# Second product with the tokens as output rows, one store for each block of tokens, squares in pairs, 64-column attention tiles, and a new order of all engines

## The chip, the cores and the metric

The kernel runs on one core of one Trainium2 chip. A core has a matrix engine (PE, with its weight loads shown apart as PEld), a vector engine (DVE), a scalar engine (ACT), a general engine (POOL) and a queue engine (SP), which here issues most of the DMA transfers. The engines run side by side and wait for each other by semaphores. The metric is the time of one execution on the device in microseconds. Names such as `h`, `r`, `g`, `o` are the program's tiles; L576 means line 576 of the kernel before.

## The reference

```python
def phi(x):                                   # r = 8 sketches, S1 and S2 are 8 x 32
    a = np.einsum('rd,bhsd->bhsr', S1, x)
    b = np.einsum('rd,bhsd->bhsr', S2, x)
    return np.einsum('bhsi,bhsj->bhsij', a, b).reshape(*x.shape[:-1], r * r)
q_p, k_p = (phi(q), phi(k))                   # batch 4, heads 4, seq 1088, head_dim 32
kv = np.einsum('bhsf,bhsd->bhfd', k_p, v)
z = np.sum(k_p, axis=2)
num = np.einsum('bhsf,bhfd->bhsd', q_p, kv)
den = np.einsum('bhsf,bhf->bhs', q_p, z)[..., None] + 1e-06
x = (num / den)                               # to 4352 tokens x 128
h = x @ w_in                                  # 128 x 2048
r = np.maximum(h, 0.0)
g = r * r
return (g @ w_out).astype(np.float32)         # 2048 x 128
```

All inputs and the output are float32. The attention is computed in float32, the two large products from bfloat16 operands.

## The kernel before

There are two parts that overlap. **Attention** goes through four batches. For each it loads k, q and v, transposes k and q on DVE (`tk`, `tq`, lines 343, 345 and 409), multiplies k with the sketches on PE (`ksk`, line 359), copies one sketch on ACT (`ka`, line 364) and multiplies the two on DVE (`kp`, line 372). `kv` (line 388) sums k features times v over the sequence in one PSUM tile; `kve` (line 401) copies the sum to SBUF. The q features of batches 0 and 1 are made in the same way (`qr` on PE, line 423; `qa` on ACT, line 435; `qp` on DVE, line 440); those of batches 2 and 3 go through DRAM: `qr` (line 452), one copy `ab` (line 459), four writes `wr`, several reads `rda` and `rdb` that spread the rows, and one DVE product (line 489). `num` (line 521) multiplies q features with `kv`, `mx` (lines 533 to 535) divides by the denominator on DVE, `tx` (line 548) transposes the quotient on PE, and `xe` (line 553) copies it to `xT`, which holds x with the 128 features as partitions and the tokens as columns.

A matrix product in float32 shows in the profile as two passes, each with a weight load of its own. The output rows of `ksk`, `kv` and `num` are cut into column tiles of 32 (`KSK_M`, `KV_M`, `NUM_M`), so that four small products stand side by side in the array.

**The two large products** go through nine blocks of tokens (384, seven times 512, 384). A block has eight steps. A step multiplies two 128-column pieces of `w_in` with the block's tokens (`m1`, line 576, two matmuls of 512 or 384 columns into an `h` tile), takes the maximum with zero (`r`, ACT line 588 or DVE line 590), squares (`g`, DVE line 603 or ACT line 601), and adds to the block's output (`m2`, line 609). In `m2` the weights `w_out` are the stationary operand and `g` streams, so the output tile `o` holds the 128 output features as partitions and the tokens as columns. `oe` (line 616) transposes 32 x 32 squares from `o` to an output tile on DVE, and four stores a block (more where a block crosses a batch), each with runs of 32 floats, bring it to DRAM (line 626).

The order is written out by hand as a table, `PLAN`: each entry names an operation, its engine and the buffers that it takes. Each engine runs its entries in the order of the table, so an entry that waits holds up all entries of its engine behind it. There are three `h` tiles, one `a`, one `o` (each in PSUM), five `r` and five `g` tiles. A transfer of the two hardware DMA queues (those that SP and ACT issue) takes one of eight semaphores in turn and so waits for the landing of the transfer eight before it. Fourteen matmuls with zeros (`heat`) fill PE at the start.

Of the kernel before, what the change touches and what calls it, by code (L numbers as in the profile page):

```python
# [44 lines left out]
ldv0.0:SP SR1:POOL heat10:PE heat11:PE heat12:PE ldv0.1:ACT ksk0.1:PE:h0 ldv1.2:SP ldv1.0:SP ka0.1:ACT tq0.0:DVE kp0.1:DVE qr0.1:PE:h1:h2 gate:POOL
ksk0.0:PE:a0 qa0.1.0:ACT:A0 qp0.1.0:DVE ka0.0:ACT qr0.0:PE:h0:h1 qa0.1.1:ACT:A1 vp0.0:POOL vp0.1:POOL kp0.0:DVE kv0.0:PE:a0 kv0.1:PE qa0.0.1:ACT:A2
qp0.0.1:DVE qp0.1.1:DVE kz0:POOL qa0.0.0:ACT:A0 ldk1.0:SP kve0.2:ACT ldv1.3:SP qp0.0.0:DVE qr0.2:PE:h1:h2 kve0.1:ACT kve0.0:DVE kz1:POOL tk1.0:DVE
ldq2.0:SP kve0.3:ACT num0.0:PE:h0 qa0.2.0:ACT:A2 num0.1:PE:a0 warm:ACT qp0.2.0:DVE mx0.0:DVE:den0 ksk1.0:PE:h1 z1:POOL tx0.0:PE:h0 heat13:PE
qa0.2.1:ACT:A1 mx0.1:DVE:den1 win1:POOL ka1.0:ACT tx0.1:PE:a0 xe0.0:ACT m1.0.2:PE:h0 win2:POOL ldv1.1:SP xe0.1:ACT win0:POOL qp0.2.1:DVE tq2.0:DVE
m1.0.3:PE:h2 ksk1.1:PE:a0 r.0.2:ACT:r0 r.0.3:ACT:r1 ldv1.t:SP qr2:PE:h0 m1.0.4:PE:h2 ldq1.0:SP kp1.0:DVE num0.2:PE:h1 ka1.1:ACT ab2:ACT r.0.4:ACT:r2  # L50
m1.0.7:PE:h0 kz3:POOL kp1.1:DVE m1.0.0:PE:h2 vp1.0:POOL kv1.0:PE:a0 wr2.2:SP r.0.7:ACT:r3 mx0.2:DVE:den2 wout0:POOL tx0.2:PE:h1 wout1:POOL
r.0.0:ACT:r4 m1.0.6:PE:h0 xe0.2:ACT g.0.4:DVE:g0 r.0.6:ACT:r2 vp1.1:POOL m1.0.1:PE:h2 m1.0.5:PE:h1 wout2:POOL g.0.2:DVE:g1 g.0.3:DVE:g2 kv1.1:PE
m1.1.4:PE:h0 g.0.0:DVE:g3 m2.0.0:PE:o0 ldv2.2:SP tq1.0:DVE r.0.1:ACT:r0 ldv2.0:SP r.0.5:ACT:r1 r.1.4:DVE:r4 g.0.1:ACT:g4 qr1.0:PE:h2:h1 m2.0.1:PE
m1.1.0:PE:h0 m2.0.2:PE m2.0.3:PE wr2.1:SP ldq3.0:SP g.0.7:DVE:g3 kve1.0:DVE qa1.0.0:ACT:A0 qa1.0.1:ACT:A2 kve1.3:DVE qp1.0.0:DVE m1.1.1:PE:h2
r.1.0:ACT:r0 g.0.5:DVE:g4 m2.0.4:PE g.0.6:ACT:g1 g.1.0:ACT:g2 qp1.0.1:DVE qr1.1:PE:h0:h1 qa1.1.0:ACT:A1 wr2.0:SP m2.0.5:PE r.1.1:DVE:r3 kve1.1:DVE
kve1.2:DVE ldv2.1:SP qa1.1.1:ACT:A0 ldk2.0:SP m1.1.2:PE:h2 num1.0:PE:a0 g.1.4:DVE:g0 r.1.2:ACT:r1 rdb2.0.1.0:SP g.1.1:ACT:g4 m2.0.6:PE qp1.1.1:DVE
# [629 lines left out]
```

## Time and profile before

| What | us |
|---|---|
| median of 3 runs | 120.26 |
| lowest and highest run | 119.08 and 120.42 |
| profiled execution, first to last instruction | 119.9 |
| PE busy | 101.0 (84%) |
| DVE busy | 94.6 (79%) |
| ACT busy | 85.0 (71%) |
| POOL busy | 15.1 (13%) |
| DMA queues issued by SP, ACT and POOL, share of 16 engines | 44.9%, 2.0%, 5.8% |

The page gives the profiled execution no other time than its span, which lies within the three runs. Busy shares are means over three stages with different limits: a head, in which the first batch's attention is loaded and computed, a long middle, in which PE works almost without a pause, and a tail with the last stores. The chain of waits follows back what ended last; rows by line give the number of instructions, their busy time and the mean duration of one; rows by stretch give the busy time of each engine within it.

### The profile page before, as it was taken

Reading aid. Unit: us, or ns where it says so; the run is one execution under the profiler, and the core shown is the slowest. Engines: PE = TensorE matmul, PEld = TensorE weight load, DVE = VectorE, ACT = ScalarE, POOL = GpSimd, SP = SyncE. Lnnn points to the kernel's source line nnn. Section 1 sums busy time; section 2 is a strip of 40 time slices with the busy share of each in tenths; the row PEclk is TensorE's granted clock in tenths of the full one; section 3 lists DMA queues with packets and bytes.
Section 4 is the critical chain, followed back from the end, with each engine's and each line's share of the span. In section 5 each row is a group of like instructions: output and inputs, shape, how many; then the busy total and the mean of one; then the engine's idle time right before and its main releaser. Section 6 shows DMA issues by size and latency. Waiting matters only on the chain.

```text
span 119.9 us, 4646 instructions
## 1 busy us (share of the span) xinstructions
PE 101.0 (84%) x2002; PEld 59.2 (49%) x2002; DVE 94.6 (79%) x154; ACT 85.0 (71%) x117; POOL 15.1 (13%) x45
## 2 busy tenths in 40 slices
...
GB/s 92 354 201 276 296 231 133 91 5 23 208 291 185 142 250 77 88 201 94 249 211 163 223 162 125 107 93 0 0 0 0 27 109 26 48 68 84 58 73 36
DMA packets 26596, 15.29 MB, mean 127 GB/s; under 512 B 19792, under 2 KB 24272, under 8 KB 26576
## 3 DMA queue, kind: packets, MB, share of 16 engines
q1 hardware_dynamic: 23808, 13.39, 44.9%
...
q10 hardware_dynamic: 1776, 0.56, 2.0%
...
HBM read 13.25 MB, written 2.79 MB: 134 GB/s over the span
## 4 chain that ended last, share of the span: by engine, by line
PE 67%; DMA 10%; issue 6%; DVE 4%; ACT 3%; ACTq 2%; SPq 1%; POOL 1%; DVEq 0%
PE h L576 24%; PE o L609 21%; DMA vin<-in_v_dram 10%; PE h L521 6%; PE a L388 4%; PE a L521 3%; PE h L548 2%; PE h L359 2%; PE h L452 2%; ACT g L601 2%; ACTq L211 2%; PE h L423 1%; ACT r L588 1%; PE a L359 1%; DVE g L603 1%
## 5 line engine op out<-in xcount | busy, mean ns | idle before, releaser
L588 ACT ACTIVATE r<-h 128x1024 bf16<-128x1024 f32 (+1 forms) x60 | 55.3, 978 | 4.2 <-PE h L576 2.5
L609 PE MATMUL o<-g,w_out 128*128 128x512 bf16 (+1 forms) x144 | 39.9, 368 | 0.7 <-DVE g L603 0.5
L576 PE MATMUL h<-xT,w_in 128*128 128x512 bf16 (+1 forms) x144 | 39.6, 369 | 0.3 <-ACT xT L553 0.2
L603 DVE TENSOR_TENSOR g<-r 128x1024 bf16<-128x1024 bf16 (+1 forms) x54 | 34.0, 670 | 0.4
L576 PEld LDWEIGHTS <-w_in 128*128 128x128 bf16 x144 | 15.6, 115 | 14.2 <-issue 1.4
L609 PEld LDWEIGHTS <-w_out 128*128 128x128 bf16 x144 | 13.3, 98 | 14.6 <-issue 1.8
L601 ACT ACTIVATE g<-r 128x1024 bf16<-128x1024 bf16 (+1 forms) x18 | 17.4, 994 | 0.6 <-PE o L609 0.4
L590 DVE TENSOR_SCALAR r<-h 128x1024 bf16<-128x1024 f32 (+1 forms) x12 | 13.7, 1153 | 0.4 <-PE h L576 0.2
L329 POOL COPY vp<-vin 128x512 f32<-128x512 f32 x8 | 5.8, 737 | 44.8 <-DMA vin<-in_v_dram 44.8
L521 PE MATMUL h<-kvz,qp 128*32 128x66 f32 x304 | 6.7, 223 | 5.1 <-issue 4.6
L521 PEld LDWEIGHTS h<-kvz,qp 128*32 128x32 f32 x304 | 5.5, 110 | 6.9 <-issue 5.8
L388 PEld LDWEIGHTS a<-vp,kp 128*32 128x32 f32 x576 | 6.3, 113 | 3.7 <-issue 3.7
L388 PE MATMUL a<-vp,kp 128*32 128x33 f32 x576 | 7.2, 202 | 0.8 <-issue 0.8
L343 DVE STREAM_TRANSPOSE kT<-kin 128x1024 f32<-128x1024 f32 (+1 forms) x5 | 5.0, 1010 | 3.4 <-DMA kin<-in_k_dram 3.4
L364 ACT COPY ka<-h 128x160 f32<-128x160 f32 (+1 forms) x4 | 1.1, 283 | 9.3 <-PE h L359 9.3
L616 DVE STREAM_TRANSPOSE osb<-o 128x512 f32<-128x512 f32 (+1 forms) x9 | 6.1, 683 | 1.7 <-PE o L609 1.7
L435 ACT COPY A<-h 128x384 f32<-128x384 f32 (+1 forms) x12 | 5.2, 462 | 2.5 <-PE h L423 2.5
L440 DVE TENSOR_TENSOR qp<-h,A 128x384 f32<-128x384 f32 (+1 forms) x12 | 6.0, 524 | 0.9 <-ACT A L435 0.9
L423 PE MATMUL h<-qT,SR 32*64 32x192 f32 (+1 forms) x192 | 6.4, 359 | 0.3 <-DVE qT L409 0.3
L359 PE MATMUL h<-SK,kT 128*32 128x64 f32 x152 | 3.5, 240 | 3.4 <-DVE SK L226 3.4
L257 PE MATMUL o<-zero 128*128 128x512 bf16 x14 | 4.8, 505 | 1.2 <-DVE zero L205 1.2
L372 DVE TENSOR_TENSOR kp<-h,ka 128x1280 f32<-128x1280 f32 (+1 forms) x4 | 5.6, 1403 | 0.0
...
## 6 DMA issues: line engine op xcount, KB each, us to landing
...
```

The source lines that it names most:

```text
L359: nc.tensor.matmul(o[m * g : m * g + m, :, j - j0, :], kT[i][:, c : c + m], SK.rearrange("p x h r -> p x (h r)"), start=True, stop=True)
L388: nc.tensor.matmul(at(vb)[p : p + m, 33 * (h // 2) : 33 * (h // 2) + 33], kp[i][:, j, 64 * h + m * f : 64 * h + m * f + m], vp[i][:, h, j, :],
L423: nc.tensor.matmul(at(hb[h // 2])[lo : lo + 64, 512 * half + 256 * x : 512 * half + 256 * x + n], SR[32 * h : 32 * h + 32, x].rearrange("p ...
L440: nc.vector.tensor_tensor(out=qp[i][:, pr, t0 : t0 + 2 * n].rearrange("p (m s) -> p m s", m=2), in0=at(hb[pr]).rearrange("p (m s) -> p m s ...
L521: nc.tensor.matmul(t[32 * cc : 32 * cc + 32 * w, 2 * pr : 2 * pr + 2, :], qp[i][:, pr, 32 * c : 32 * c + 32 * w], (kvs if sw else kvz)[b][ ...
L576: nc.tensor.matmul(at(hb)[:, col(w) : col(w) + N], w_in[:, 512 * (ct // E) : 512 * (ct // E) + 512].rearrange("p (c e) -> p e c", e=E)[:, ...
L588: nc.scalar.activation(o, i_, ACTF.Relu)
L590: nc.vector.tensor_scalar_max(o, i_, 0.0)
L601: nc.scalar.activation(at(gb)[:, 0:tot], r, ACTF.Square)
L603: nc.vector.tensor_tensor(out=at(gb)[:, 0:tot], in0=r, in1=r, op=ALU.mult)
L609: nc.tensor.matmul(at(ob)[:, 0:N], w_out[:, ct, :], at(gb)[:, W * N * (mm % SQ_W) + N * w : W * N * (mm % SQ_W) + N * w + N], start=(ct == ...
L616: nc.vector.transpose(at(sbuf)[:, 0:N], at(ob)[:, 0:N])
```

## The change

In `m2` the operands change places: pieces of 128 tokens of `g` become the stationary operand and `w_out` streams, 128 columns at a time. One matmul of 512 columns becomes four of 128 columns, each with a weight load of its own, and the output tile has tokens as partitions. `m1` reads the tokens in another sequence (runs of 32 columns), chosen so that a partition of the output tile holds neighbouring rows of the output. `oe` becomes a plain copy on ACT or DVE, and a block is stored by one transfer with runs of up to 2 KB (a few where a block crosses a batch) instead of four or more with runs of 128 B. Squares of the seven 512-token blocks are taken over two steps at once (2048 columns), with four `r` tiles and three `g` tiles of twice the size. The column tiles of `ksk`, `kv` and `num` are 64 wide. The sketches are the first loads of ACT's queue, v of batch 0 is loaded by SP, and one of the two small sketch copies moves from POOL to ACT. The table `PLAN` is new for all engines.

```diff
--- before.py
+++ after.py
@@ -16,14 +16,15 @@
 N_H = 3
 N_A = 1
 N_O = 1
-NR = 5
-SQ_W = 1
-N_OSB = 4
+N_R = 4
+N_G = 3
+SQ_W = (1, 2, 2, 2, 2, 2, 2, 2, 1)
+N_OSB = 3
 N_DEN = 3
 N_AA = 3
 N_HEAT = 14
-NUM_M = (32, 32, 32, 32)
-S_ENG = "ACT"
+NUM_M = (64, 64, 64, 64)
+S_ENG = "ACT|SP"
 W_PARTS = ((0, 1), (1, 2), (2, 4))
 MODE = ('pe', 'pe', 'dma', 'dma')
 Q_LOADS = (((0, 12), (12, 34)), ((0, 34),), ((0, 34),), ((0, 34),))
@@ -32,63 +33,57 @@
 KVS = (((0, 4), (4, 9)), ((0, 4), (4, 9)), ((0, 4), (4, 9)), ((0, 4), (4, 9)))
 RD_PARTS = (((0, 768), (768, 1088)), ((0, 768), (768, 1088)), ((0, 768), (768, 1088)), ((0, 768), (768, 1088)))
 SIZES = [384, 512, 512, 512, 512, 512, 512, 512, 384]
-KSK_M = (32, 32, 32, 32)
-KV_M = (32, 32, 32, 32)
+KSK_M = (64, 64, 64, 64)
+KV_M = (64, 64, 64, 64)
 V_ENG = "SP|ACT"
 RDB_ENG = "SP"
+ST_ENG = "SP"
 K_LOADS = (((0, 16), (16, 34)), ((0, 34),), ((0, 34),), ((0, 34),))
 
 
 PLAN = """
-iota:POOL ldv0.3:ACT zero:DVE heat0:PE:o0 heat1:PE heat2:PE heat3:PE z0:POOL mk:POOL heat4:PE lds1:ACT ldk0.16:SP tk0.16:DVE ldk0.0:SP lds0:ACT
...
+zero:DVE heat0:PE:o0 heat1:PE heat2:PE z1:POOL kz2:POOL mk:POOL ldq0.0:SP tq0.0:DVE lds1:ACT lds0:ACT trS:DVE ldk0.16:SP tk0.16:DVE ldk0.0:SP SK:DVE
...
 """
 
 
@@ -150,9 +145,9 @@
         tiles[f"a{i}"] = PS(f"a{i}", 512)
     for i in range(N_O):
         tiles[f"o{i}"] = PS(f"o{i}", 512)
-    for i in range(NR):
-        tiles[f"r{i}"] = T(f"r{i}", [128, 1024 * SQ_W], BF16)
-        tiles[f"g{i}"] = T(f"g{i}", [128, 1024 * SQ_W], BF16)
+    for kind, count in (("r", N_R), ("g", N_G)):
+        for i in range(count):
+            tiles[f"{kind}{i}"] = T(f"{kind}{i}", [128, 1024 * max(SQ_W)], BF16)
     for i in range(N_OSB):
         tiles[f"osb{i}"] = T(f"osb{i}", [128, 512])
     for i in range(N_DEN):
@@ -560,12 +555,14 @@
         last = None
         W = 4 if N <= 256 else 2
         per = 512 // N if N <= 256 else 1
+        sq = SQ_W[n]
+        X = N // 128
         for m in range(CT // W):
-            if m % SQ_W == 0:
+            if m % sq == 0:
                 rb, gb = Buf("r"), Buf("g")
                 o_r = []
             hb = Buf("h")
-            off = W * N * (m % SQ_W)
+            off = W * N * (m % sq)
 
             def col(w, N=N, per=per):
                 return 512 * (w // per) + N * (w % per)
@@ -576,7 +573,7 @@
                     nc.tensor.matmul(
                         at(hb)[:, col(w) : col(w) + N],
                         w_in[:, 512 * (ct // E) : 512 * (ct // E) + 512].rearrange("p (c e) -> p e c", e=E)[:, ct % E],
-                        xT[:, n0 : n0 + N], start=True, stop=True)
+                        xT[:, n0 : n0 + N].rearrange("p (c x t) -> p x c t", x=X, t=32), start=True, stop=True)
             wi = o_win[wpart(W * m + W - 1)]
             wo = o_wout[wpart(W * m + W - 1)]
             o1 = add(f"m1.{n}.{m}", "PE", f_m1, deps + [wi], alloc=[hb], n=W * N)
@@ -588,12 +585,12 @@
                     nc.scalar.activation(o, i_, ACTF.Relu)
                 else:
                     nc.vector.tensor_scalar_max(o, i_, 0.0)
-            new = m % SQ_W == 0
+            new = m % sq == 0
             o_r.append(add(f"r.{n}.{m}", "ACT|DVE", f_r, [o1], alloc=[rb] if new else [], uses=[hb] if new else [hb, rb], n=W * N,
                            after=[] if new else o_r[:1]))
-            if m % SQ_W < SQ_W - 1:
+            if m % sq < sq - 1:
                 continue
-            tot = W * N * SQ_W
+            tot = W * N * sq
 
             def f_g(e, rb=rb, gb=gb, tot=tot):
                 r = at(rb)[:, 0:tot]
@@ -602,32 +599,42 @@
                 else:
                     nc.vector.tensor_tensor(out=at(gb)[:, 0:tot], in0=r, in1=r, op=ALU.mult)
             o3 = add(f"g.{n}.{m}", "DVE|ACT", f_g, o_r, alloc=[gb], uses=[rb], n=tot)
-            for mm in range(m - SQ_W + 1, m + 1):
+            for mm in range(m - sq + 1, m + 1):
                 def f_m2(e, mm=mm, gb=gb):
                     for w in range(W):
                         ct = W * mm + w
-                        nc.tensor.matmul(at(ob)[:, 0:N], w_out[:, ct, :],
-                                         at(gb)[:, W * N * (mm % SQ_W) + N * w : W * N * (mm % SQ_W) + N * w + N],
-                                         start=(ct == 0), stop=(ct == CT - 1))
+                        lo = W * N * (mm % sq) + N * w
+                        for x in range(X):
+                            nc.tensor.matmul(at(ob)[:, 128 * x : 128 * x + 128], at(gb)[:, lo + 128 * x : lo + 128 * x + 128], w_out[:, ct, :],
+                                             start=(ct == 0 and x == 0), stop=(ct == CT - 1), skip_group_check=True)
                 last = add(f"m2.{n}.{mm}", "PE", f_m2, [o3, wo, last], alloc=[] if mm else [ob], uses=[gb, ob] if mm else [gb], n=W * N)
         sbuf = Buf("osb")
 
         def f_oe(e):
-            nc.vector.transpose(at(sbuf)[:, 0:N], at(ob)[:, 0:N])
-        o_oe = add(f"oe{n}", "DVE", f_oe, [last], alloc=[sbuf], uses=[ob], n=N)
-        lo = n0
-        while lo < n0 + N:
-            b = lo // S
-            hi_ = min(n0 + N, S * (b + 1))
-            c0, c1 = (lo - S * b) // 32, (hi_ - S * b) // 32
-            for db in range(4):
-                def f_st(e, db=db, lo=lo, hi_=hi_, b=b, c0=c0, c1=c1):
-                    en = nc.sync if e == "SP" else nc.scalar
-                    en.dma_start(
-                        out=out[S * b : S * b + S, :].rearrange("(t c) d -> t c d", c=C)[:, c0:c1, 32 * db : 32 * db + 32],
-                        in_=at(sbuf)[32 * db : 32 * db + 32, lo - n0 : hi_ - n0].rearrange("p (c d) -> p c d", d=32))
-                add(f"st{n}.{lo}.{db}", "SP|ACT" if n == len(SIZES) - 1 else "SP", f_st, [o_oe], uses=[sbuf], n=128 * (hi_ - lo))
-            lo = hi_
+            fn = nc.scalar.copy if e == "ACT" else nc.vector.tensor_copy
+            fn(at(sbuf)[:, 0:N], at(ob)[:, 0:N])
+        o_oe = add(f"oe{n}", "DVE|ACT", f_oe, [last], alloc=[sbuf], uses=[ob], n=N)
+        c0, runs = n0 // 32, []
+        for g in range(4):
+            lo = c0 + X * g
+            while lo < c0 + X * g + X:
+                hi_ = min(c0 + X * g + X, C * (lo // C + 1))
+                if hi_ - lo == X and runs and runs[-1][3] - runs[-1][2] == X * runs[-1][1] and runs[-1][3] % C:
+                    runs[-1][1] += 1
+                    runs[-1][3] = hi_
+                else:
+                    runs.append([g, 1, lo, hi_])
+                lo = hi_
+        for i, (g, k, lo, hi_) in enumerate(runs):
+            def f_st(e, g=g, k=k, lo=lo, hi_=hi_):
+                en = {"SP": nc.sync, "ACT": nc.scalar, "POOL": nc.gpsimd}[e]
+                b, w = lo // C, (hi_ - lo) // k
+                x0 = lo - c0 - X * g
+                en.dma_start(
+                    out=out[S * b : S * b + S, :].rearrange("(t c) d -> t c d", c=C)[:, lo - C * b : hi_ - C * b].rearrange(
+                        "t (k x) d -> k t (x d)", k=k),
+                    in_=at(sbuf)[32 * g : 32 * g + 32 * k, 128 * x0 : 128 * x0 + 128 * w])
+            add(f"st{n}.{i}", ST_ENG if n < len(SIZES) - 1 else "SP|ACT", f_st, [o_oe], uses=[sbuf], n=16384 * (hi_ - lo))
 
     for b in range(B):
         attention(b)
@@ -635,7 +642,7 @@
     for n, N in enumerate(SIZES):
         ffn(n, n0, N)
         n0 += N
-    assert n0 == N_TOK
+    assert n0 == N_TOK and len(SQ_W) == len(SIZES)
 
     if not PLAN.strip():
         raise Planless(ops, slots)
```

How the order moves is shown at three places. The first is ACT's queue at the start; `S_sb` holds the sketches, `vin` is v of batch 0. Before:

```order
L314 DMA vin_114<-in_v_dram 32x4x256
L211 DMA S_sb<-in_S_dram 64x1x32 x2
L314 DMA vin_114<-in_v_dram 32x4x256 x2
L364 ACT_TABLE_LOAD
L364 COPY ka_128<-h_63 128x160
```

And in the changed kernel:

```order
L206 DMA S_sb<-in_S_dram 64x1x32 x2
L230 ACT_TABLE_LOAD
L230 COPY SR<-ST 128x64
L430 COPY A_87<-h_65 128x384
L430 COPY A_88<-h_63 128x384
```

The sketch loads now stand ahead of everything on ACT, and the three loads of v have left it for SP. The second place is DVE ahead of the first division `den`, `rec`, `xs`, on which the first `m1` depends (`kp` are the k features, `qp` the q features, `kT` and `qT` the transposed inputs). Before:

```order
L440 TENSOR_TENSOR qp_138<-h_65,A_92 128x384
L440 TENSOR_TENSOR qp_138<-h_63,A_91 128x384
L401 COPY kvz_132<-a_66 64x2x33
L343 STREAM_TRANSPOSE kT_123<-kin_107 128x1024
L345 STREAM_TRANSPOSE kT_123<-kin_107 128x64
L440 TENSOR_TENSOR qp_138<-h_64,A_93 128x320
L533 TENSOR_SCALAR den_82<-h_63 128x12
L534 RECIPROCAL rec_83<-den_82 128x12
L535 TENSOR_TENSOR xs_84<-h_63,rec_83 128x384
```

And in the changed kernel:

```order
L367 TENSOR_TENSOR kp_126<-a_66,ka_124 128x1024
L435 TENSOR_TENSOR qp_134<-h_63,A_88 128x320
L404 STREAM_TRANSPOSE qT_121<-qin_107 128x1088
L435 TENSOR_TENSOR qp_134<-h_64,A_89 128x384
L435 TENSOR_TENSOR qp_134<-h_65,A_87 128x384
L404 STREAM_TRANSPOSE qT_120<-qin_108 128x1088
L216 TENSOR_SCALAR ident<-iot 128x128
L528 TENSOR_SCALAR den_78<-a_66 128x12
L529 RECIPROCAL rec_79<-den_78 128x12
L530 TENSOR_TENSOR xs_80<-a_66,rec_79 128x384
```

The transposes of q of batches 1 and 2 and the making of `ident` now stand ahead of the first division, and the transpose of k of batch 1 has moved behind it. The third place is the end of SP's queue, the last stores (`osb` are the output tiles). Before:

```order
L626 DMA out_dram<-osb_79 32x8x32
L626 DMA out_dram<-osb_78 32x16x32 x4
L626 DMA out_dram<-osb_81 32x6x32
L626 DMA out_dram<-osb_79 32x8x32 x4
L626 DMA out_dram<-osb_80 32x12x32
```

And in the changed kernel:

```order
L633 DMA out_dram<-osb_75 32x512
L633 DMA out_dram<-osb_75 2x32x512
L633 DMA out_dram<-osb_76 4x32x512
L633 DMA out_dram<-osb_75 32x256
L633 DMA out_dram<-osb_77 4x32x384
```

Eleven stores of 32-float runs, with three more on ACT's queue, stand at the end before; in the changed kernel five stores of long runs do, and the last block's is a single one.

More of the change, by code (lines that the diff above doesn't have):

```diff
@@ L45 @@
[L45 to L56, printed above, removed]
@@ new lines @@
+iota:POOL win0:POOL ident:DVE kve0.1:ACT kve0.3:ACT kve0.0:ACT kve0.2:ACT num0.0:PE:a0 mx0.0:DVE:den0 qa1.1.1:ACT:A2 qp1.1.1:DVE qr2:PE:h2 heat11:PE
+heat12:PE wout0:POOL win1:POOL qa1.1.0:ACT:A0 qp1.1.0:DVE tk1.0:DVE ab2:ACT wr2.3:SP tx0.0:PE:a0 xe0.0:ACT qr1.2:PE:h1:h2 ldv1.0:SP ldv1.3:SP
+qa1.2.1:ACT:A1 qp1.2.1:DVE qa1.2.0:ACT:A2 ldv1.2:SP qp1.2.0:DVE heat13:PE m1.0.0:PE:h0 ksk1.0:PE:a0 r.0.0:ACT:r3 ka1.0:ACT kp1.0:DVE g.0.0:DVE:g0
+m1.0.4:PE:h2 r.0.4:ACT:r0 ksk1.1:PE:h1 ldv1.1:SP ka1.1:ACT m1.0.7:PE:h0 r.0.7:ACT:r1 m1.0.3:PE:h2 r.0.3:ACT:r2 kp1.1:DVE num0.1:PE:a0 mx0.1:DVE:den0
@@ new lines @@
+m1.0.2:PE:h0 r.0.2:ACT:r3 m2.0.0:PE:o0 num0.2:PE:h2 mx0.2:DVE:den1 qr1.0:PE:h0:h1 g.0.4:ACT:g1 qa1.0.0:ACT:A0 qp1.0.0:DVE kz3:POOL vp1.0:POOL
+kv1.0:PE:a0 ldv1.t:SP vp1.1:POOL qa1.0.1:ACT:A1 kv1.1:PE m1.0.1:PE:h2 qp1.0.1:DVE g.0.3:ACT:g2 kve1.0:DVE kve1.1:ACT kve1.3:ACT kve1.2:ACT tx0.2:PE:h0
+xe0.2:DVE r.0.1:ACT:r2 tx0.1:PE:h1 xe0.1:ACT num1.1:PE:a0 g.0.1:ACT:g0 m1.0.6:PE:h0 r.0.6:ACT:r0 ldk2.0:SP m1.0.5:PE:h2 r.0.5:ACT:r2 wr2.1:SP
+ldq3.0:SP num1.0:PE:h1 m2.0.1:PE g.0.2:ACT:g0 ldv2.0:SP wr2.0:SP tq3.0:DVE qr3:PE:h0 ab3:ACT mx1.1:DVE:den2 mx1.0:DVE:den1 m1.1.0:PE:h2 wr2.2:SP
@@ new lines @@
+wout1:POOL m2.0.2:PE g.0.7:DVE:g0 tk2.0:DVE r.1.0:ACT:r3 m1.1.2:PE:h1 r.1.2:ACT:r1 num1.2:PE:a0 mx1.2:DVE:den0 m1.1.3:PE:h0 r.1.3:ACT m1.1.1:PE:h2
+tx1.0:PE:h1 xe1.0:DVE m2.0.3:PE g.0.5:ACT:g2 r.1.1:ACT wout2:POOL m2.0.4:PE m1.1.6:PE:h0 rda2.0.1:SP m1.1.4:PE:h1 r.1.4:ACT:r2 ldv3.t:SP ldv2.2:SP
+g.0.6:DVE:g1 m2.0.5:PE rdb2.768.1.1:SP r.1.6:DVE:r0 ldv2.1:SP rdb2.0.1.0:SP ldv2.3:SP vp2.0:POOL m2.0.6:PE rda2.0.0:SP wr3.0:SP ldk3.0:SP m2.0.7:PE
+oe0:DVE:osb1 tx1.1:PE:a0 xe1.1:ACT m1.1.5:PE:h2 wr3.2:SP ldv3.3:SP r.1.5:ACT g.1.1:DVE:g1 m1.2.4:PE:h0 rdb2.0.0.0:SP tx1.2:PE:h1 xe1.2:ACT ldv2.t:SP
```

65 lines of the change are left out of this document (29 added, 36 removed).

## The prediction

> **What bounds the kernel now.** I read the page first (span), then the busy time by stretch, then the chain of waits.
>
> ```profile
> span 119.9 us, 4646 instructions
> ...
> 0.00:18.00 18.00, 12.18 (x350) 7.43 (x350) 8.91 (x17) 4.63 (x13) 7.89 (x32) 0.91 0.86 241
> 18.00:21.53 3.53, 0.00 (x1) 0.01 (x2) 0.95 (x3) 0.41 (x2) 1.84 (x5) 0.96 0.94 129
> ...
> 25.48:105.44 79.96, 78.44 (x1510) 45.19 (x1510) 75.25 (x117) 73.68 (x95) 5.34 (x9) 1.00 0.49 117
> 105.44:112.71 7.27, 6.59 (x34) 3.12 (x32) 6.32 (x10) 5.51 (x7) 0.00 (x0) 1.00 0.48 82
> ```
>
> A row by stretch has its length, then PE, PEld, DVE, ACT and POOL busy, the granted clock, and the DMA share with its GB/s. From 25.48 to 105.44 PE works 78.44 of 79.96 us (98%), DVE 94%, ACT 92%: the middle is PE's. The head is 25.48 us long, and 7.2 us are left of the span after the last matmul at 112.71. The chain of waits says what holds the head:
>
> ```profile
> 17.35 0.65 PE h L521 x25
> 18.00 3.53 issue
> ...
> 24.95 0.49 ACT xT L553
> 25.48 0.81 PE h L576 x4
> ```
>
> The first `m1` starts at 25.48, as soon as its 384 tokens of x are there. Ahead of it PE stands still for 3.53 us in the middle of `num`, and "issue" means that no wait in the profile explains it. I read it as PE waiting for its own code, since 350 matmuls had been run by then and the DMA engines were at 94% in those 3.53 us; this is a reading, not shown. Earlier, the timeline shows the sketches late:
>
> ```profile
> 0.74 0.42 ACTq L314 DMA_DIRECT2D vin<-in_v_dram  x1
> 1.19 1.84 ACTq L211 DMA_DIRECT2D S_sb<-in_S_dram  x2
> ...
> 8.09 0.21 DVE L224 STREAM_TRANSPOSE ST<-S_sb 128x32 f32<-128x32 f32 x1 [2.72 <-DMA S_sb<-in_S_dram]
> ```
>
> Their issue ends at 3.03 and DVE gets them at 8.09, 5.06 us later; all of `ksk`, `qr` and `kp` stand behind.
>
> **The head.** The sketch issue, 1.84 us long, now starts at 0.74 and ends at 2.58. With the old 5.06 us they would land at 7.6; with the shortest landing of any store row below, 1.6 us from issue, at 4.2. No load is ahead of them on ACT any more, so I take 5.0, nearer to the short end. From there DVE decides, because nearly all steps up to the first division stand on it:
>
> ```profile
> L372 DVE TENSOR_TENSOR kp<-h,ka 128x1280 f32<-128x1280 f32 x3 | 4.4, 1475 | 0.0
> L372 DVE TENSOR_TENSOR kp<-a,ka 128x1024 f32<-128x1024 f32 x3 | 3.7, 1218 | 0.1
> L440 DVE TENSOR_TENSOR qp<-h,A 128x384 f32<-128x384 f32 x8 | 4.2, 550 | 0.9 <-ACT A L435 0.9
> L440 DVE TENSOR_TENSOR qp<-h,A 128x320 f32<-128x320 f32 x4 | 1.8, 471 | 0.0
> L409 DVE STREAM_TRANSPOSE qT<-qin 128x1088 f32<-128x1088 f32 x3 | 3.9, 1301 | 0.0
> L409 DVE STREAM_TRANSPOSE qT<-qin 128x704 f32<-128x704 f32 x1 | 0.9, 905 | 0.0
> L343 DVE STREAM_TRANSPOSE kT<-kin 128x512 f32<-128x512 f32 x2 | 1.4, 691 | 3.4 <-DMA kin<-in_k_dram 3.4
> L535 DVE TENSOR_TENSOR xs<-h,rec 128x384 bf16<-128x384 f32 x4 | 2.2, 558 | 0.1
> ```
>
> In the new order DVE runs behind the sketches: their transpose 0.21, two k transposes 1.38, three small ones (0.6 together, my allowance), `qp` 4 x 0.55 and 2 x 0.47, q transposes 0.91 and 2 x 1.30, `kp` 1.48 and 1.22, then the division, 0.56 and two short steps (0.4, allowance). That is 12.5 us, so 17.5 without a wait. One microsecond for hand-overs from PE and ACT, and about 0.8 for `tx` and `xe` (the 0.49 above and three transposes) put the first `m1` at 19.3, say **19.0 to 19.5**. `kv` lies under it. It also needs `w_in`, which POOL issues only after v of batch 0:
>
> ```profile
> 0.00:9.05 9.05, 4.44 (x13) 1.56 (x14) 2.08 (x8) 1.28 (x1) 1.80 (x15) 1.00 0.70 215
> ...
> DMA to landing us min/median/max: 5.7/6.3/7.7
> ```
>
> At 215 GB/s the 1.65 MB of S, q, k and v are in by 7.7; a microsecond for the landing, about 2 for POOL's copies of v, 0.6 for each of two issues, then 5.7 to 7.7 (the row is `w_in`'s): 17.6 to 19.6. The two conditions meet, so no slack is left. The code wait: ahead of its first `m1` the new order has 325 matmul passes against 460 (counted in the order, heat included), because the tiles are wider, fewer than the 350 after which PE stood still. If it comes back it comes behind the first `m1`, and I count nothing. The clock is no term: 1.00 granted in the whole middle.
>
> **The second product.** The weights of `m2` now change with every matmul. The nearest row for a matmul of 128 columns with a weight load of its own is the transpose `tx`, six in a row:
>
> ```profile
> 84.84 0.54 PEld L548 LDWEIGHTS <-xs 128*128 128x128 bf16 x6
> ...
> 85.06 0.50 PE L548 MATMUL h<-ident,xs 128*128 128x128 bf16 x6
> 85.39 0.59 PE L609 MATMUL o<-g,w_out 128*128 128x512 bf16 x2
> ...
> 85.98 0.86 PE h L576 x4
> ...
> 103.13 0.33 PE h L576 x2
> ...
> L609 PEld LDWEIGHTS <-w_out 128*128 128x128 bf16 x144 | 13.3, 98 | 14.6 <-issue 1.8 <-DVE osb L616 0.9
> ```
>
> From 85.06 to 85.39 are 0.33 us for six: 56 ns each, weight loads included. 512 columns take 0.86 / 4 = 215 ns and 384 take 165 ns. So `m2` goes from 112 x 0.215 + 32 x 0.165 = 29.4 to 544 x 0.056 = 30.5 us: **+1.1**, on PE and so on the path. If the loads, 98 ns each, were not hidden, it would be 544 x 0.098 = 53.3, +23.9 (a rival). The Trainium skill ("TensorE: Matmul & The Clock Gate", section "Back-to-back issue gap") speaks against the change here: it gives about 81 ns for each 128-column matmul in a sustained stream of load and matmul, which would make 44.1 us, an estimate of +14.7. The six in a row do not show that, but six are no stream. The new token sequence of `m1` (runs of 32 columns) has no row; I take 0.
>
> **The tiles of 64.** Passes (two for each float32 product) fall from 1440 to 736. What a pass takes:
>
> ```profile
> 62.80 0.56 PE h L359 x40
> ...
> 53.68 0.69 PE a L388 x60
> ...
> 39.08 0.83 PE a L521 x48
> ```
>
> `ksk` with 64 columns takes 14.0 ns, `kv` with 33 takes 11.5, `num` with 66 takes 17.3. The time grows with the columns, so it is mostly the array's, and a tile twice as wide fills it twice as long. A line through 33 and 66 leaves 5.7 ns that may belong to the instruction: 704 fewer passes would save 4.0 us. Against it stand the longer weight loads; these rows bound them:
>
> ```profile
> L423 PEld LDWEIGHTS h<-qT,SR 32*64 32x64 f32 x192 | 4.0, 144 | 1.7 <-issue 1.1 <-ACT r L588 0.3 <-DVE kp L372 0.2
> L388 PEld LDWEIGHTS a<-vp,kp 128*32 128x32 f32 x576 | 6.3, 113 | 3.7 <-issue 3.7
> ```
>
> 64 columns 31 ns more than 32, two tiles side by side: 736 x 0.031 / 2 = 11 us if none is hidden. Most is, as under `tx`. Range -4 to +4, taken at **-1**.
>
> **Squares and copies.** Rows of DVE and of an ACT copy out of PSUM:
>
> ```profile
> L603 DVE TENSOR_TENSOR g<-r 128x1024 bf16<-128x1024 bf16 x43 | 28.5, 701 | 0.4
> L603 DVE TENSOR_TENSOR g<-r 128x768 bf16<-128x768 bf16 x11 | 5.6, 548 | 0.0
> L435 ACT COPY A<-h 128x384 f32<-128x384 f32 x8 | 3.5, 481 | 2.5 <-PE h L423 2.5
> ```
>
> 256 columns more cost 153 ns, so a pair costs 0.70 + 1024 x 0.0006 = 1.31 instead of 1.40, 28 times: 2.5 us over DVE and ACT. Six of nine output copies leave DVE for ACT, where 384 columns take 0.48 us; 512 take some 0.6 (allowance), so ACT gets about 3.5. Neither engine carries the end now, so both are worth 0 on the path; the cover is PE's 98%. The pair has a price too: the first step's half waits for the second.
>
> **The middle.** From the first `m1` to the last `m2` before: 112.71 - 25.48 = 87.2. Add 1.1 (`m2`) and -1 (tiles). Work changes sides of the first `m1`: `num` (0.83) and `ksk` (0.45) move behind it, three `qr` groups (2.5, at 0.8 each, allowance) ahead of it: -1.2. The parts of `w_out` that POOL issues behind v of batch 1, the pairs, and ACT busy at once with maxima and squares cost waits that I put at +2 (0 to 4). Sum 88.1.
>
> **The tail.** The last rows:
>
> ```profile
> 112.75 0.58 DVE L616 STREAM_TRANSPOSE osb<-o 128x384 f32<-128x384 f32 x1 [0.90 <-PE o L609]
> 113.37 1.38 ACTq L626 DMA_DIRECT2D out_dram<-osb  x3
> 115.03 2.29 SPq L626 DMA_DIRECT2D out_dram<-osb  x5
> ...
> DMA to landing us min/median/max: 1.6/1.9/3.8
> ```
>
> SP issues five stores up to 117.32, and the span ends 2.59 later. Now: copy 0.48, hand-overs 0.1, one issue of about 0.4, then 2.59, and 0.8 for 192 KB instead of 48 (allowance): 4.4 instead of 7.2, **-2.8**.
>
> **Sum.** 19.3 + 88.1 + 4.4 = 111.8. Against the profiled 119.9 that is -8.1; the median of the runs is 0.36 above the profiled span, which makes 112.2. Rounded, **112**.
>
> **Rivals.** (1) The head gains only half: PE's code wait comes back behind the first `m1`, or `w_in` lands late. For it: the DMA engines are still busy with weights then, and PE stood still in `num`. Against: fewer passes. +3.5: 115.5. Chance 0.20. (2) Slower: the weight loads of `m2` set its pace. For it: 98 ns a load, 544 of them. Against: six transposes at 56. It decides where the 8.1 us are used up, at (30.5 + 8.1) / 544 = 71 ns; above that the kernel is slower than before. At 98 ns 112 + 22.8 = 134.8. By the Trainium skill's 81 ns it would be about 126, an estimate. Chance 0.09. (3) The pairs starve PE: with three `g` tiles and three `h` tiles PE waits 0.2 us at each of 28 pairs, +5.6: 117.6. Chance 0.10, since ACT and DVE are at 92 and 94%. (4) The head does not move, because loads and not the order hold it; then only the tail and `m2` count: 119.9 - 2.8 + 1.1 = 118.2. Chance 0.06. My forecast: 0.55.
>
> **Numbers.** About 1% (1.2 us) is what a measurement of this kernel can tell from no change; so faster means under 119.1. Cases forecast, 1 and 3 are faster, most of 4 too: 0.86. Same 0.05, from the ends of 3 and 4. Slower 0.09. Low end: tiles -4 instead of -1 and no waits, 112 - 5 = 107. High end 117.5, the third case; above it remain 2, most of 4, in all about 0.15.
>
> **What would show it.** First `m1` at 19 to 19.5 and no idle "issue" over 1 us ahead of it (else rival 1); `m2`'s matmuls 56 ns apart in a run of eight (else 2); PE over 96% busy in the middle (else 3); the sketch transpose near 5 us (else 4); 4.4 us from the last matmul to the end. A first `m1` after 22 or a pace over 71 ns would make the prediction wrong.

## The result: slower, 124.4 us, where 112 was forecast

| | before | changed kernel |
|---|---|---|
| median of the runs, us | 120.34 (4 runs) | 124.44 (4 runs) |
| ratio to before, 95% interval | | 1.038 [1.030, 1.045] |
| the same, run again later on another chip | 121.61 (19 runs) | 123.40 (4 runs), 1.027 [1.010, 1.044] |
| profiled span, us | 119.9 | 122.6 |
| first `m1`, us | 25.48 | 22.36 |
| first `m1` to last `m2`, us | 87.2 | 93.8 |
| last `m2` to the end, us | 7.2 | 6.4 |

Here and below, ratios compare the executions that ran undisturbed, while medians are of all, so a ratio can differ from that of the medians beside it. The head gained 3.1 us, about half of what was forecast, the tail 0.8 in place of 2.8, and the middle, which was to grow by 0.9, grew by 6.6.

The chain of waits of the changed kernel, start and length in us:

```profile
22.36 0.33 PE h L573 x2
...
28.91 2.22 PE a L383 x72
...
60.16 1.80 PE o L608 x32
...
65.55 8.61 DMA Bq<-scr
...
98.42 8.04 DMA out_dram<-osb
...
106.54 0.59 ACT osb L615
...
116.19 0.48 ACT osb L615
```

Two DMAs of over 8 us stand on the chain, where the middle before was almost PE's alone. The first brings `Bq` of batch 3, for which a `qp` step on DVE waits; the second is a store: the copy of block 6 on ACT (106.54) wants an output tile whose store isn't done. What they cost PE is in its timeline, the wait and who ended it in brackets (the product at 77.22 also needs a square that DVE made from 75.95 to 77.17, behind the `qp` step that had waited for `Bq`):

```profile
77.22 0.95 PE L608 MATMUL o<-w_out,g 128*128 128x128 bf16 x14 [2.01 <-ACT r L585]
...
107.17 1.00 PE L608 MATMUL o<-w_out,g 128*128 128x128 bf16 x15 [1.85 <-ACT osb L615]
```

By stretch (length, then PE, PEld, DVE, ACT and POOL busy, granted clock, DMA share, GB/s), the middle and the tail:

```profile
22.36:116.17 93.81, 89.48 (x1374) 68.17 (x1371) 76.10 (x102) 77.07 (x98) 7.43 (x14) 0.98 0.41 115
116.17:122.60 6.43, 0.00 (x0) 0.00 (x0) 0.00 (x0) 0.58 (x2) 0.00 (x0) 0.79 0.17 53
```

PE stands still for 4.33 us of the middle, and the clock granted is 0.98 of full speed. Now the transfers of the stretch in which the second DMA is awaited. The first row has the busy share of the 16 DMA engines in tenths, in 40 slices of 0.2 us:

```profile
DMA  0000027006011124122222222222222222222211
...
DMA packets 262, 0.52 MB, mean 65 GB/s; under 512 B 7, under 2 KB 7, under 8 KB 262
...
out_dram<-osb SPq DMA_DIRECT2D x2, 256.0 KB
```

Two stores are under way, nothing else, and from 102 us on a steady two tenths of the engines work. The row by stretch gives this, and an earlier stretch, a number:

```profile
90.00:96.00 6.00, 6.00 (x92) 4.92 (x93) 5.47 (x8) 4.57 (x6) 0.00 (x0) 1.00 0.11 36
99.00:106.00 7.00, 6.26 (x68) 4.51 (x66) 6.76 (x6) 4.82 (x5) 0.00 (x0) 1.00 0.24 74
```

From 90 to 96 us the stores of shape 2x32x512 run: 0.11 of 16 is 1.8 engines. From 99 to 106 it is those of 4x32x512: 0.24 of 16 is 3.8. A store seems to get as many engines as its outermost dimension counts, 2 or 4, and two stores at once share the same ones. The stores before, with 32 tokens outermost, had no such limit; this is the same row for the kernel before from 100 to 112 us, where its transfers are nearly all stores, with up to nine tenths:

```profile
DMA  0000000000071943414326334372343609347758
```

That is the first theory. The Trainium skill ("DMA: Bandwidth & Descriptors", section "Why a DMA increments its semaphore by 16 and not by 1") states it as a rule: a DMA runs on the largest number up to 16 that divides the slowest dimension of both its sides, and one issued from SP takes the lowest-numbered engines; both shares agree. The rivals: too few output tiles, or an order of stores that keeps a tile too long (the store of block 3 is issued after that of block 5), whatever their speed.

### The profile page after: what moved, and what is told of

It is laid out like the page before. It is cut to its first block, busy times and chain, and to the rows that moved or that the text cites. A ratio compares the mean times of both kernels' runs of the same rounds, so it can differ in the third digit from the quotient of the medians.

```text
span 122.6 us, 3954 instructions
## 1 busy us (share of the span) xinstructions
PE 106.0 (86%) x1696; PEld 78.0 (64%) x1698; DVE 90.2 (74%) x126; ACT 85.2 (70%) x118; POOL 14.3 (12%) x44
## 4 chain that ended last, share of the span: by engine, by line
PE 60%; DMA 17%; issue 5%; ACT 5%; DVE 4%; SPq 2%; ACTq 1%; DVEq 0%
PE o L608 17%; PE h L573 16%; DMA Bq<-scr 7%; DMA out_dram<-osb 7%; PE a L516 5%; PE h L516 4%; PE h L418 3%; DMA S_sb<-in_S_dram 3%; PE a L354 3%; PE o L252 2%; PE a L383 2%; ACT r L585 2%; PE h L383 2%; PE h L447 2%; DVE g L600 1%
## 5 line engine op out<-in xcount | busy, mean ns | idle before, releaser
L608 PE MATMUL o<-w_out,g 128*128 128x128 bf16 x544 | 37.2, 219 | 3.9 <-ACT r L585 2.0
L608 PEld LDWEIGHTS <-g 128*128 128x128 bf16 x544 | 32.9, 98 | 11.2 <-DVE g L600 2.7
L600 DVE TENSOR_TENSOR g<-r 128x2048 bf16<-128x2048 bf16 (+1 forms) x33 | 34.2, 1061 | 5.2 <-ACT r L585 2.7
L598 ACT ACTIVATE g<-r 128x768 bf16<-128x768 bf16 (+1 forms) x11 | 12.4, 1136 | 0.3 <-PE o L608 0.2
L367 DVE TENSOR_TENSOR kp<-a,ka 128x1024 f32<-128x1024 f32 (+1 forms) x6 | 7.8, 1302 | 0.8 <-ACT ka L359 0.8
L484 DVE TENSOR_TENSOR qp<-qp,Bq 128x1536 f32<-128x1536 f32 (+1 forms) x4 | 5.1, 1284 | 4.0 <-DMA Bq<-scr 4.0
L383 PEld LDWEIGHTS a<-vp,kp 128*64 128x64 f32 x216 | 6.7, 138 | 1.7 <-issue 1.5
L383 PE MATMUL a<-vp,kp 128*64 128x33 f32 x216 | 7.1, 224 | 0.3 <-DVE kp L367 0.3
L404 DVE STREAM_TRANSPOSE qT<-qin 128x1088 f32<-128x1088 f32 (+2 forms) x5 | 5.4, 1075 | 2.0 <-DMA qin<-in_q_dram 2.0
L516 PE MATMUL a<-kvz,qp 128*64 128x66 f32 (+1 forms) x96 | 5.3, 251 | 0.3 <-ACT kvs L396 0.3
```

Source lines behind the costliest of these rows:

```text
L367: nc.vector.tensor_tensor(out=oo.rearrange("p (m x y) -> p m x y", x=R, y=R), in0=bb.rearrange("p (m y) -> p m y", y=R)[:, :, None, :].to_ ...
L383: nc.tensor.matmul(at(vb)[p : p + m, 33 * (h // 2) : 33 * (h // 2) + 33], kp[i][:, j, 64 * h + m * f : 64 * h + m * f + m], vp[i][:, h, j, :],
L516: nc.tensor.matmul(t[32 * cc : 32 * cc + 32 * w, 2 * pr : 2 * pr + 2, :], qp[i][:, pr, 32 * c : 32 * c + 32 * w], (kvs if sw else kvz)[b][ ...
L598: nc.scalar.activation(at(gb)[:, 0:tot], r, ACTF.Square)
L600: nc.vector.tensor_tensor(out=at(gb)[:, 0:tot], in0=r, in1=r, op=ALU.mult)
L608: nc.tensor.matmul(at(ob)[:, 128 * x : 128 * x + 128], at(gb)[:, lo + 128 * x : lo + 128 * x + 128], w_out[:, ct, :], start=(ct == 0 and x ...
```

## The experiments

**Stores cut by groups.** One DMA for each group of 32 partitions, so that 32 tokens are outermost:

```
-                en.dma_start(
-                    out=out[...].rearrange("(t c) d -> t c d", c=C)[:, lo - C * b : hi_ - C * b].rearrange(
-                        "t (k x) d -> k t (x d)", k=k),
-                    in_=at(sbuf)[32 * g : 32 * g + 32 * k, 128 * x0 : 128 * x0 + 128 * w])
+                for kk in range(k):
+                    en.dma_start(
+                        out=out[...].rearrange("(t c) d -> t c d", c=C)[
+                            :, lo - C * b + w * kk : lo - C * b + w * kk + w].rearrange("t x d -> t (x d)"),
+                        in_=at(sbuf)[32 * (g + kk) : 32 * (g + kk) + 32, 128 * x0 : 128 * x0 + 128 * w])
```

> The changed kernel, with every store of an output tile cut into one DMA for each 32-partition group (1, 2 or 4 of them in place of one), so that the token, of which there are 32, is the outermost dimension of each; bytes, 2048-byte or 1536-byte packets, order of the engines and buffers stay. Theory 1, few engines per store: in the changed kernel two stores of two groups kept only 0.11 of the 16 engines busy (90 to 96 us) and two of four groups 0.24 (99 to 106 us), so a store goes at the pace of as many engines as its outermost dimension counts. Then the two waits of the chain (for Bq at 74.3 us, for the output tile at 106.5 us) go or shrink below 1 us, the stores come in the windows with a share above 0.4, and from the last matmul to the end it takes about 4.4 us in place of 6.4: 2.5 + 4 to 6 + 2 us less, 113 to 116 us. Theory 2, the buffers and the planned order are at fault (three output tiles, eight turns of DMA semaphores), or SP gets late by the more issues (some 20 more at about 0.06 us, and their waits): the waits stay, and it takes 122 to 126 us.

Measured: 117.69 us against 121.99 of before, ratio 0.964 [0.958, 0.970], 6 to 7% better than the changed kernel (1.027 and 1.038). Its middle and tail, and its transfers in the same stretch of 8 us:

```profile
22.73:110.87 88.14, 87.52 (x1374) 67.05 (x1371) 76.11 (x102) 76.91 (x98) 8.24 (x14) 1.00 0.45 124
110.87:115.80 4.93, 0.00 (x0) 0.00 (x0) 0.00 (x0) 0.58 (x2) 0.00 (x0) 0.76 0.16 40
```

```profile
DMA  3916500000000000000000332816638100300000
...
out_dram<-osb SPq DMA_DIRECT2D x4, 64.0 KB, 1.7
```

Stores now come in bursts and land 1.7 us after their issue, and no wait for an output tile is left. The wait for `Bq` is shorter, not gone: 3.51 us of it stay on the chain, and DVE stands for 1.75 us in place of 3.99 ahead of `qp`, where the first theory had under 1 us; but PE hardly waits for it any more. The span falls by 6.8 us: 3.7 of PE's idle time in the middle (0.62 left), 2.0 of its busy time for the same matmuls (the clock is 1.00 in place of 0.98), 1.5 in the tail, less 0.4 for a later head. The number of output tiles and the order of the stores are as they were, so neither is the whole cause, and the first theory holds. The further issues did not hold up SP enough to show, though one takes some 0.42 us and not the 0.06 us of the expectation.

**Five output tiles, the stores unchanged.**

```
-N_OSB = 3
+N_OSB = 5
-    vtl = [T(f"vtl{i}", [32, H, 2, D]) for i in range(B)]
+    vtl_all = T("vtl_all", [128, H, 2, D])
+    vtl = [vtl_all[32 * i : 32 * i + 32] for i in range(B)]
...
-... oe6:ACT:osb0 ...
+... oe6:ACT:osb1 ...
```

> The changed kernel with five output tiles in place of three, taken in turn, the stores unchanged (one DMA for 1, 2 or 4 groups, the group outermost). Theory 1, few engines per store: the stores stay as slow, the copy of the seventh block does not wait for a tile any more, but the wait for Bq near 74 us stays and the last store still ends more than 6 us after the last matmul: 4 to 6 us less than the changed kernel, 118 to 121 us. Theory 2, too few output tiles are the whole loss: 113 to 116 us, as good as the run with the stores cut by groups or better.

Measured: 122.04 us, ratio 1.002 [0.994, 1.009]. The copy of block 6 waits no more, but in the chain stands

```profile
67.70 7.96 DMA Bq<-scr
...
114.27 0.48 ACT osb L616
```

and the span ends at 120.8, 6.5 us after the last product. PE's idle time in the middle is 2.2 us in place of 4.3. Too few tiles are a part of the second wait and of nothing else; the median came out a little above what the first theory gave (118 to 121 us).

**Which stores.** The changed kernel with the cut for some blocks only, blocks 0 to 2 and, in a second run, blocks 3 to 8:

```
+                if n <= 2:
+                    for kk in range(k):
+                        en.dma_start(... one group of 32 partitions ...)
+                else:
                     en.dma_start(... k groups ...)
```

with `if n >= 3:` in the second.

> The changed kernel with the stores of blocks 0 to 2 alone cut by groups (those ahead of the Bq reads near 63 to 73 us); the later ones as changed. If the early stores cause the wait for Bq and the late ones the wait for the output tile and the long end: the chain's wait for Bq falls to about 3.5 us as in the run with all cut, the wait for the output tile (near 8 us on the chain) and the 6 us from the last matmul to the end stay. 2 to 4 us less than the changed kernel, and with the other half it adds up to what all cut gave.

> The changed kernel with the stores of blocks 3 to 8 alone cut by groups; those of blocks 0 to 2 as changed. The wait for Bq near 74 us stays (about 8 us on the chain), the wait for the output tile goes, and from the last matmul to the end it takes 4.9 us in place of 6.4: 3 to 5 us less than the changed kernel. If the waits do not add up (one hides behind the other), this run or the one with the early stores cut is as good as all cut.

Measured, beside the unaltered changed kernel at 1.027: early ones cut 1.014 [1.000, 1.027], late ones cut 0.996 [0.986, 1.006]. Each has one of the two DMAs left in its chain. Early cut:

```profile
94.95 7.97 DMA out_dram<-osb
```

Late cut:

```profile
66.90 8.43 DMA Bq<-scr
```

With the early ones cut, `Bq` leaves the chain altogether. PE's idle time in the middle, by stretch as above, is 4.1 us in the changed kernel on this chip, 2.0 with the early and 2.4 with the late ones cut, and was 0.6 with all cut: in PE's idle time the two waits add up. The loss of 2.7% becomes 1.4 and -0.4%: the late ones gain 3 to 4 us, as expected, the early ones some 1.6 us, less than the 2 to 4 expected. The two gains together, 4.5%, leave 0.982, where all cut had measured 0.964 on another chip; with intervals of 0.6 to 1.7% each, that gap can't be called one. So the early stores, which stand ahead of `Bq` in SP's queue, held it up; the late ones held the output tile and the end.

**Each store in two halves, the group still outermost.** Twice the DMAs, with the same few engines: this tells the outermost count from the number of DMAs.

```
+                for x1, x2 in (((0, 2), (2, w)) if k > 1 else ((0, w),)):
                     en.dma_start(
-                        ... "t (k x) d -> k t (x d)", k=k),
+                        ... "t (k x) d -> k t x d", k=k)[:, :, x1:x2].rearrange("k t x d -> k t (x d)"),
-                        in_=at(sbuf)[32 * g : 32 * g + 32 * k, 128 * x0 : 128 * x0 + 128 * w])
+                        in_=at(sbuf)[32 * g : 32 * g + 32 * k, 128 * (x0 + x1) : 128 * (x0 + x2)])
```

> The changed kernel with each store of 2 or 4 groups cut into two DMAs by token order within a group (2 + 2 or 2 + 1 of its columns), the group still the outermost dimension of each, stores of one group as they were: twice the DMAs, packets of 1024 and 512 bytes, the same outermost counts of 2 and 4. Theory 1, the outermost count sets how many engines a store gets: two DMAs of one store share the same 2 or 4 engines, so both waits of the chain stay and the time is as the changed kernel's or worse, 1.03 to 1.06 of the kernel before. Theory 2, one DMA was too few at a time and more DMAs fill more engines: as when the stores were cut by groups, 0.96 to 0.985.

Measured: 1.000 [0.994, 1.006]. That fitted neither, so the changed kernel and this one were run side by side.

> The changed kernel itself, unaltered, beside the three other runs of this call, because the run with each store in two halves came out at 1.00 of the kernel before where the changed kernel had been 1.04. If that difference is of the chip or of the measurement, it comes to 1.00 to 1.01 here, as the halves do; if the halves did gain, it is at 1.03 to 1.05 again.

> The run with each store in two halves (group still outermost, twice the DMAs), again, beside the changed kernel. In its trace the two stores of four groups moved at 92 to 102 GB/s with 2 tenths of the engines busy, as in the changed kernel. Theory 1 (the outermost count sets the engines): within 0.5 us of the changed kernel. Theory 2 (more DMAs, more engines): 3 to 5 us less than it.

Measured: the changed kernel 1.027 [1.010, 1.044], the halves 1.004 [0.996, 1.012]. The transfers of the halves, from 98 to 106 us:

```profile
DMA  2212222222222332222222222222221000000000
...
out_dram<-osb SPq DMA_DIRECT2D x2, 128.0 KB
```

Still two tenths of the engines: more DMAs do not fill more engines. Yet halves gained some 2% (the two intervals just touch), where the first theory allowed 0.5 us. On the chain the wait for the store is 5.9 us in place of 8.0 and that for `Bq` 6.3 in place of 6.8, and PE's idle time in the middle is 1.8 us in place of 4.1. So the outermost count is not all that sets how long these stores hold others up; why halves help is left open.

**The tiles of 64 columns.** All three products on 32 columns again, with the stores cut; then the key-value products alone, in all batches (`KV_M` alone at 32), and in the last two only (`KV_M = (64, 64, 32, 32)`):

```
-NUM_M = (64, 64, 64, 64)
+NUM_M = (32, 32, 32, 32)
-KSK_M = (64, 64, 64, 64)
-KV_M = (64, 64, 64, 64)
+KSK_M = (32, 32, 32, 32)
+KV_M = (32, 32, 32, 32)
```

> The changed kernel with its stores cut by groups, and with the attention on tiles of 32 columns again (sketch products, key-value products and numerators; nothing else). A batch of key-value products took 2.22 us on 64 columns and 1.66 us on 32. Theory 1, the 64-column tiles cost PE that: four times 0.56 us and about as much as 0.2 us a batch in sketch products come back, 2 to 3 us less than the run that has the stores cut alone. Theory 2 (the prediction's term: the tiles gain 1 us): 0.5 to 1.5 us more than that run. Theory 3: the engine plan hides either, within 0.5 us.

> The changed kernel with its stores cut by groups, and the key-value products alone on tiles of 32 columns again in all four batches (sketch products and numerators stay on 64). Without it the same kernel was at 0.964 of the kernel before; with all three kinds on 32 columns PE stood still for 2.1 us in the numerators of batch 0 and for 3.8 us in the middle of the key-value products of batch 1, for nothing that the profile shows. Theory 1, PE waits for its code, and the passes added decide how long: key-value products of 32 columns add 288 passes where all three kinds add 704; a shorter stop of 0 to 2.5 us returns near the key-value products of batch 1, and PE gets back 4 x 0.6 us in those products: 0.955 to 0.975 of the kernel before. Theory 2, the stops come from something else (loads, the sketch and numerator tiles): no stop, 0.944 to 0.950 (2.3 us less).

> The changed kernel with its stores cut by groups, and the key-value products of batches 2 and 3 alone on tiles of 32 columns (1.6 us each in place of 2.2 us). Theory 1, PE waits for its code only while the loads of the head are under way, and is the bound in the middle: no stop, PE saves 2 x 0.6 us, so 1.0 to 1.2 us less than the run with the stores cut alone: 0.952 to 0.957 of the kernel before. Theory 2, every pass more costs a stop wherever it stands, or the two batches are not on the path: 0.961 or more.

Measured: all on 32, a median of 125.45 us (lowest 122.62), against 117.69 (lowest 116.57) with the stores cut alone; key-value products on 32, 124.43 (lowest 122.64); the last two batches, 117.77, ratio 0.968 [0.958, 0.978]. None of the first run's three theories held: not 2 to 3 us less, but some 5 to 6 more. The chain of the run with all on 32 shows where:

```profile
32.94 0.65 PE a L383 x53
33.59 3.83 issue
```

PE stops in the middle of a row of matmuls for 3.83 us and waits for nothing that the profile shows. The run with only the key-value products on 32 stops at the same place (PE's timeline), and in the transfers of those 3.5 us there is one of the queue that brings code:

```profile
33.26 0.98 PE L383 MATMUL a<-vp,kp 128*32 128x33 f32 x63 [2.89 <-issue]
```

```profile
q8 instruction: 1, 0.02, 2.1%
```

2.1% of 16 engines in 3.5 us are 1.18 us of one engine for that packet. In the trace it starts at 30.6, so it ends near 31.8, and PE goes on at 33.26, 1.5 us later. Much the same time lies between the end of a code packet and the end of other such stops: in the run with all on 32 (packet over at 35.95, PE on at 37.41), in this one at 60.3 (58.8), and in the run with the last two batches:

```profile
52.98 1.53 PE L383 MATMUL h<-vp,kp 128*32 128x33 f32 x144
...
57.24 0.69 PE L354 MATMUL a<-SK,kT 128*64 128x64 f32 x16 [1.46 <-issue]
```

Here batch 2 took 1.5 us in place of 2.2, and PE then stood for 1.46 us. In the traces of all runs, behind the first 6 us, there are eleven stops of PE of more than 0.7 us that no wait explains, and each ends 1.3 to 1.6 us after a code packet has; stops as long that do have a named wait end 6 us or more after one. Three of the eleven are in the kernel before: the 3.53 us from 18.00, which the prediction read so without proof, end 1.4 us after a packet that was over at 20.17. So the first theory of the run with key-value products on 32 fits, at an undersized price (stops of 2.89 and 2.46 us, and one of 1.40 ahead of them, where 0 to 2.5 us in all were expected), and the one of the last run is wrong in that the stop stays away outside the head. The Trainium skill ("Runtime: NRT & Kernel Launch", section "Instruction fetch mechanics") says that code comes in blocks of 16 KiB, fetched while the present one runs, and calls the cost mostly hidden; the packet has that size, but here the cost isn't hidden. That the stop is the wait for this packet, and that many short passes use code up faster than it comes, is argued from the times; no run moved a packet alone.

**The clock-keeping matmuls of the head.** Without `heat5` to `heat9`, 2.25 us on the chain between the first query and key products, and the stores cut:

```
-N_HEAT = 14
+N_HEAT = 9
-... qr0.0:PE:h2:h0 qa0.0.0:ACT:A0 heat5:PE heat6:PE ldv0.0:SP heat7:PE heat8:PE heat9:PE
+... qr0.0:PE:h2:h0 qa0.0.0:ACT:A0 ldv0.0:SP
```

> The changed kernel with its stores cut by groups and without the five clock-keeping matmul groups (heat5 to heat9) that stand on PE between the first query product and the first key product; they lay on the chain for 2.25 us. Theory 1: they hold up the first key product: the first m1 comes 1 to 2 us earlier than 22.4 us, and the time falls by 1 to 2 us against the run that has the stores cut alone. Theory 2: they hide behind the arrival of the key rows (PE would wait that long anyway) or keep the clock up: the first m1 within 0.4 us of 22.4 or later, the time the same or up to 1 us longer.

Measured: 117.26 us, 0.961 [0.955, 0.968], not to be told from the cut alone (0.964). From the sketches' transpose to the first `m1` it takes 15.0 us (7.83 to 22.85) in place of 16.3 (6.47 to 22.73), so the groups do cost 1.2 us on that way; but the sketches happened to land 1.4 us later in that execution. In the traces of the changed kernel and its variants they land between 5.9 and 7.8 us. The granted clock stayed at 1.00 without these groups. Whether the time gains a microsecond stays open.

**The three edits together**: stores cut, no `heat5` to `heat9`, the last two batches' key-value products on 32.

> The three edits together: stores cut by groups, the five clock-keeping groups ahead of the first key product left out, and the key-value products of batches 2 and 3 on 32 columns. If each acts as in its own run, 0.9614 less 1.0 to 1.2 us: 0.950 to 0.955 of the kernel before. If the clock-keeping groups matter for the clock, a granted clock below 0.98 and 0.96 or more.

Measured: 117.36 us, 0.962 [0.950, 0.975]. No gain that can be told from the cut alone: in the middle PE stands still for 1.2 us, against 0.2 without the tiles of 32, and 0.75 us of it is one more stop behind a code packet (over at 55.50, PE on at 56.82). The version with the stores cut by groups, with or without those clock-keeping groups, is the one to keep: it beats both kernels.

## Why the prediction was wrong

- **The stores: the step that failed.** The forecast priced the new stores once, as 0.8 us for 192 KB at the end, an allowance, and the other stores not at all. Measured, the span ends 5.4 us behind the last issue, where 2.59 and 0.8 were put, and in all the slow stores and what hangs on them are worth 6.8 us of span: 3.7 idle, 2.0 by the clock of that execution (which the forecast put at nothing), 1.5 in the tail, against 0.4 that the head lost. The shapes 2x32x512 and 4x32x384 stood in the order that was shown. The row of landing times used for the end (1.6 to 3.8 us) came from stores with 32 tokens outermost, and was carried over to another shape. None of the rivals named it; the one that ends slower was weight loads, and the forecast's range ended at 117.5.
- **The tail.** With the stores cut it is 4.93 us against the forecast 4.4: the size was right for stores on all engines, and the cut adds three issues of about 0.43 us each. In the changed kernel it was 6.43.
- **The second product: right.** 32 matmuls in 1.80 us and 24 in 1.34 are 56 ns each, as the six transposes had it, and the loads are hidden. By the Trainium skill's 81 ns ("TensorE: Matmul & The Clock Gate", section "Back-to-back issue gap") 32 would have taken 2.6 us, an estimate; in this kernel's streams the shorter time stands, and the second rival falls.
- **The tiles: the choice was right, the term was not.** The sum of -1 came from 4 us saved in passes against longer weight loads. Measured, a batch of key-value products takes 2.22 us with 72 passes of 64 columns, 31 ns a pass, more than the 1.5 to 1.6 us with 144 of 32: +0.6 a batch. Half the passes gained nothing in the others either: `ksk` takes 0.73 us for 20 (before 0.56 to 0.69 for 40), `num` 0.85 for 24 (before 0.83 for 48). Weight loads that are not hidden would do that; no run separates them. What the wide tiles bring is fewer stops: with all three products on 32 columns the kernel is some 5 to 6 us slower, stops of 2.1 and 3.8 us among them. The forecast had the code wait only as a way for the head to gain less, in the first rival.
- **Squares and copies: right.** A pair took 1.22 us against 1.31 forecast, and PE waits 0.6 us in the whole middle with the stores cut, where +2 was allowed. The third rival falls.
- **The middle.** 88.1 us were forecast, and 88.14 measured once the stores are cut; by luck, since the waits were put 1.4 us too high and the tiles too low by about as much.
- **The head: half.** First `m1` at 22.36 in place of 19.3, past the 22 us that the forecast itself had named as a sign of being wrong; with the 3.1 us gained the fourth rival falls. DVE's rows tell where the 3.1 us went:

```profile
6.04 0.21 DVE L219 STREAM_TRANSPOSE ST<-S_sb 128x32 f32<-128x32 f32 x1 [2.31 <-DMA S_sb<-in_S_dram]
...
8.75 1.02 DVE L435 TENSOR_TENSOR qp<-h,A 128x384 f32<-128x384 f32 x2 [1.05 <-ACT A L430]
...
11.67 1.49 DVE L367 TENSOR_TENSOR kp<-h,ka 128x1280 f32<-128x1280 f32 x1 [1.08 <-ACT ka L359]
...
19.50 0.17 DVE L528 TENSOR_SCALAR den<-a 128x12 f32<-128x12 f32 x1 [0.66 <-PE a L516]
...
19.97 0.56 DVE L530 TENSOR_TENSOR xs<-a,rec 128x384 bf16<-128x384 f32 x1
```

  The sketches came 1.0 us late. From there to the end of the division it took 14.5 us in place of 13.5: DVE's work was a microsecond shorter than summed, but the hand-overs, put at 1 us, were 3 (the three brackets, and 0.2 more). And behind the division it took 1.8 us, not 0.8, because PE does a query group (0.82 us) and two clock-keeping matmuls before the first `m1`. The first rival's 3.5 us are nearly met in size, but by neither of its causes: no stop of PE's code and no late `w_in` is on the chain. (The chain has an `issue` of 1.73 us at 15.79, but it is ACT's; PE runs the 72 passes of `kv` from 15.15 to 17.44 without a pause.)

So the mechanism in second product and squares was right, in the head in part, and the unpriced stores turned a gain into a loss. With the stores mended the kernel measures 117.7 us beside 122.0 of before on its chip: the sign forecast, about half of the gain. Of the 4 us of span that are missing to the forecast's 111.8, the head is 3.4 and the tail 0.5.
